# Sliding-window attention with sink keys and a swish feed-forward on one core: q and k put in token order by the read of PSUM, sink keys written by GpSimd, new constants in the planner

## The chip, the cores and the metric

One core of a Trainium2 chip runs the whole program. The metric is the device time of one execution in microseconds, on the slowest core; here there is only one. Five engines work side by side: TensorE (PE, with its weight load PEld), VectorE (DVE), ScalarE (ACT), GpSimd (POOL) and the queue engine SP, which here only issues DMAs. POOL and, once at the start, ACT issue DMAs too.

## The reference

Attention with 4 batches, 8 heads, 768 tokens and head size 64. A query sees the 4 first keys (the sinks) and the 128 keys up to itself. The result goes, token by token with all heads side by side, into a two-layer feed-forward.

```python
scores = scale * np.matmul(q, k.transpose(0, 1, 3, 2))
keep = is_sink | in_window
a = np.exp(np.where(keep, scores, -1e9) - max); a = a / a.sum()
x = (a @ v).transpose(0, 2, 1, 3).reshape(3072, 512)
h = x @ w_in                         # 512 -> 2048
g = h * (1.0 / (1.0 + np.exp(-beta * h)))
out = g @ w_out                      # 2048 -> 512
```

## The kernel before

The tokens are cut into 8 half-batches of 384 tokens (hb 0 to 7; two make a batch). A unit `u` is one pair of heads in one half-batch, so there are 32 units, 4 in each half-batch. The steps of a unit, each a function of `_program`:

- `load` and `cast`: q, k and v come by DMA as float32 and are cast to bf16 (`x16`, `vaug`) by DVE and ACT in hb 0, by POOL from then on. In the load of q and k a partition holds three consecutive tokens, so column block j of the cast tile holds the tokens 3s+j.
- `T` (line 420): six 128x128 transposes on PE put q and k of the unit into one PSUM bank, 768 columns of bf16 in the order (q or k, j, s). One copy (line 433, on ACT or DVE, whichever the planner holds to be free sooner) takes them to `qkT` in SBUF in token order (s, j): it reads the bank column by column and writes with a step of three elements. In an even half-batch two small copies by the same engine (line 440) put the 4 sink keys of each head into `kS`, a weight tile that is zero elsewhere: head 0 in the upper 64 rows at column 0, head 1 in the lower 64 rows at column 32.
- `SC` and `SS`: scores of the window blocks (8 matmuls over 4 banks) and of the sinks (one matmul with `kS` as weights); ACT takes the exponential (lines 489, 516), POOL masks the diagonal blocks with selects (line 495), DVE the sink block (line 503).
- `AV`: the weighted sum of v with a column of ones for the denominator; DVE divides (lines 555, 557, tile `onorm`). `OT`: three transposes back, copied to `xT` by ACT or DVE.

The feed-forward has 128 steps `H` (line 589: four matmuls of 384 columns, then tanh on ACT at line 593 and a product on DVE at line 595) and 96 steps `O` (line 607: four matmuls of 512 columns; every fourth ends a tile of 128 tokens, which is copied to `osb` and stored). An H step of a half-batch needs all four units of it.

The weights `w_in` and `w_out` come in four pieces each, by DMAs that POOL issues (line 384); all other loads are issued by SP. Loads are kept in order by `ordered`: a load waits until the load that lies `AHEAD_BYTES` back in the list `LOADS` has landed.

The order of everything is laid down when the program is built. `Graph` keeps a clock for each engine, `add` puts every instruction at a planned time from the cost that its caller gives (`act_ns`, `dve_ns`, `pool_ns`, `mm_ns`) and adds 180 ns where it waits for another engine. The loop at the end of `_program` (line 728) asks at each step which of OT, AV, SC, SS, T, H and O could start on PE, in this order, and takes the first that is ready by the planned clock, or else the one that is ready soonest. `background` (line 688) issues loads while the planned end of the DMAs is less than `BACKLOG` ahead, and casts. On the chip each engine then runs its instructions in that order and waits on semaphores.

Of the kernel before, what the change touches and what calls it, by code (L numbers as in the profile page):

```python
# [4 lines left out]
BF16 = mybir.dt.bfloat16  # L5
F32 = mybir.dt.float32
AF = mybir.ActivationFunctionType
ALU = mybir.AluOpType

B, H, S, D = 4, 8, 768, 64  # L10
NSINK, WINDOW = 4, 128
# [6 lines left out]
HALF = S // 2  # L18
# [209 lines left out]
def _program(nc, G, sb, ps, q, k, v, w_in, w_out, beta, out):  # L228
    NU = 2 * NPAIR
    NSTG, NX, NV, NT, NE, NON, NG, NTT, NOS, NKS = 2, 2, 3, 8, 3, 3, 3, 3, 4, 4  # L230
    NK = NB // 2
    ident = sb("ident", (128, 128), BF16)
    ones = sb("ones", (128, 128), BF16)
# [2 lines left out]
    ident32 = sb("ident32", (16, 16), F32)  # L236
    hbeta = sb("hbeta", (128, NM), F32)
    warm = sb("warm", (1, 1), F32)
    xT = sb("xT", (128, 4, NTOK), BF16)
    w_in16 = sb("w_in16", (128, 4, DF), BF16)  # L240
    w_out16 = sb("w_out16", (128, NM, NOUT), BF16)
# [5 lines left out]
    qkT = sb("qkT", (128, 2, HALF), BF16, NT)  # L247
    E = sb("E", (128, 6, 2, 128), BF16, NE)
    ES = sb("ES", (128, HALF), BF16, NE)
    kS = sb("kS", (128, 128), BF16, NKS)  # L250
# [8 lines left out]
    def add(eng, fn, ns, r=(), w=(), x=(), dma=None):  # L259
        return G.add(eng, fn, ns, r, w, x, dma)  # L260

    AHEAD_BYTES = 1600000

    def mm_ns(n):
        return max(n / 2.4, 25) + 3
# [30 lines left out]
    def take(n):  # L296
        got = choose(n)[1]
        held.update(got)
        return got
# [8 lines left out]
    def copy_fn(eng, dst, src, scale=1.0):  # L308
        if eng == "dve":
            if scale == 1.0:  # L310
                return lambda e: e.tensor_copy(dst, src)  # L311
            return lambda e: e.tensor_scalar(dst, src, scale, None, ALU.mult)
        return lambda e: e.activation(dst, src, AF.Copy, bias=0.0, scale=scale)  # L313


    def consts():
        add("gp", lambda e: e.memset(ones[:, :], 1.0), 150, w=["ones"])
        add("gp", lambda e: e.affine_select(ident[:, :], ones[:, :], [[1, 128]], ALU.is_equal, 0.0,
                                            base=0, channel_multiplier=-1), 250, r=["ones"], w=["ident"])
        add("gp", lambda e: e.affine_select(ident32[:, :], ones[0:16, 0:16], [[1, 16]], ALU.is_equal, 0.0,  # L320
                                            base=0, channel_multiplier=-1), 150, r=["ones"], w=["ident32"])
        for i in range(NV):
            add("gp", lambda e, i=i: e.memset(vaug[i][:, :, :, D:D + 1], 1.0), 50, w=[("vones", i)])
        for i in range(NKS):
            add("gp", lambda e, i=i: e.memset(kS[i][:, :], 0.0), 80, w=[("kS", i)])
        for i in range(2):
            add("gp", lambda e, i=i: e.memset(vS[i][:, :, :], 0.0), 350, w=[("vS", i)])
        for i, sg in ((0, 1), (1, -1)):
            add("gp", lambda e, i=i, sg=sg: e.affine_select(
                maskS[:, i, :], ones[:, :], [[sg, 128]], ALU.is_ge, 0.0, base=min(sg, 0), channel_multiplier=-sg),  # L330
                250, r=["ones"], w=[("maskS0", i)])
        add("gp", lambda e: e.affine_select(maskS[:, :, :], maskS[:, :, :], [[0, 2], [0, 128]], ALU.is_ge, 1.0,
                                            base=-NSINK, channel_multiplier=1), 400,
            r=[("maskS0", 0), ("maskS0", 1)], w=["maskS"])

        add("act", lambda e: e.activation(warm[:, :], ones[0:1, 0:1], AF.Exp, bias=0.0, scale=1.0), 1300,
            r=["ones"], w=["warm"])
# [12 lines left out]
    def ordered(nbytes):  # L350

        ahead, wait = 0, []
        for key, b_ in reversed(flight):
            ahead += b_
            if ahead > AHEAD_BYTES:
                wait = [key]
# [63 lines left out]
    def T(u):  # L420

        hb, hp = u // 4, u % 4
        bs = take(1)
        mp = P[:, bs[0], :].bitcast(BF16)
        for i, n in enumerate("qk"):
            for c in range(NK):
                add("pe", lambda e, i=i, n=n, c=c: nc.tensor.transpose(  # L427
                    mp[:, i * HALF + c * 128:i * HALF + (c + 1) * 128],
                    x16[n][hb % NX][:, c, 2 * hp:2 * hp + 2, :].rearrange("p h d -> p (h d)"), ident[:, :]),
                    mm_ns(128), r=[(n + "16", hb % NX, hp, c), "ident"], x=[("B", bs[0])])  # L430
        opts = {"dve": dve_ns(2 * HALF), "act": act_ns(2 * HALF)}
        eng = quickest(opts)
        add(eng, copy_fn(eng, qkT[u % NT][:, :, :].rearrange("p a (s j) -> p a j s", j=NK),
                         mp[:, 0:2 * HALF].rearrange("p (a j s) -> p a j s", a=2, j=NK)), opts[eng],
            w=[("qkT", u % NT)], x=[("B", bs[0])])
        if hb % 2 == 0:
            ks = u % NKS
            for hh in range(2):
                rows = slice(64 * hh, 64 * hh + 64)
                add(eng, copy_fn(eng, kS[ks][rows, 32 * hh:32 * hh + NSINK], qkT[u % NT][rows, 1, 0:NSINK]), 70,  # L440
                    r=[("kS", ks), ("qkT", u % NT)], w=[("kSd", ks, hh)])
        give(bs)


# [62 lines left out]
    def SS(u):  # L507

        b, half, hp = where(u)
        z, ks = u % NE, (u - 4 * half) % NKS  # L510
        q0 = 0 if half else 256
        bs = take(1)
        add("pe", lambda e: e.matmul(P[:, bs[0], q0:HALF], kS[ks][:, :], qkT[u % NT][:, 0, q0:HALF], start=True,  # L513
                                     stop=True), mm_ns(HALF - q0),
            r=[("kSd", ks, 0), ("kSd", ks, 1), ("qkT", u % NT)], x=[("B", bs[0])])
        add("act", lambda e: e.activation(ES[z][:, q0:HALF], P[:, bs[0], q0:HALF], AF.Exp, bias=0.0, scale=SCALE),  # L516
            act_ns(HALF - q0), w=[("ES", z)], x=[("B", bs[0])])
        give(bs)
# [113 lines left out]
    HS = [(T_, m) for T_ in range(NSB) for m in range(NM)]  # L632
    OS = [(T_, t, j) for T_ in range(NSB) for t in range(3) for j in range(4)]
    n_cast = [0]
    BACKLOG, AHEAD = 3000, 300

    def head(s):

# [89 lines left out]
    while True:  # L728
        background()
        now = G.free["pe"]  # L730
        if not started and done["T"] >= 2:
            beta_in()
            started = True
        ffn = ("O", "H") if last == "H" else ("H", "O")
        best = None
        for s in ("OT", "AV", "SC", "SS", "T") + ffn:
            h = head(s)
            if h is None:
                continue
            if h[0] <= now:  # L740
                best = (now, s, h[1])
                break
            if best is None or h[0] < best[0]:
                best = (h[0], s, h[1])
        if best is None:
            if done["O"] == len(OS):
                break
            G.free["pe"] = now + 200
            assert now < 1e6, (done, n_cast)
            continue  # L750
        _, s, fn = best
        if best[0] > now + 200:
            G.free["pe"] = now + 200
            continue
        fn()
        done[s] += 1
        if s in ("H", "O"):
            last = s
# [33 lines left out]
```

## Time and profile before

| what | us |
|---|---|
| median of 3 runs (lowest, highest) | 263.96 (263.18, 267.93) |
| the profiled execution | 265.0 |
| its span, first to last instruction | 263.2 |
| PE busy in it | 234.8 |
| ACT busy in it | 179.1 |
| DVE busy in it | 132.6 |
| POOL busy in it | 100.5 |

The 1.8 us between the profiled execution and its span lie outside the instructions. A busy PE is not a PE at its best rate: matmuls overlap, and the record of each is longer than the step from one to the next. So a stretch is read by the step between rows that follow one another, and by what stands at the same place when nothing is waited for.

### The profile page before, as it was taken

To read this page: it belongs to the slowest core of one execution; us is meant where nothing else is said; L and a number is where in the kernel's file an instruction comes from. 1 tells how busy PE (TensorE), PEld (TensorE's weight loads), DVE (VectorE), ACT (ScalarE), POOL (GpSimd) and SP (SyncE) were. 2 spreads that over 40 slices of the span, in tenths; PEclk is the share of its full clock that TensorE was granted. 3 is DMA by queue.
4 is the path that set the end of the run, shared out by engine and by line. 5 is a ranking of instruction groups with operands and counts; after the bars stand their busy time and mean duration, and the time that the engine had idled before them with its cause. 6 is when DMAs were issued, how large, how long until landed. Compare 5 with 4: busy or idle time off the path is not lost.

```text
span 263.2 us, 4995 instructions
## 1 busy us (share of the span) xinstructions
PE 234.8 (89%) x1889; PEld 132.6 (50%) x1889; DVE 132.6 (50%) x267; ACT 179.1 (68%) x307; POOL 100.5 (38%) x202
## 2 busy tenths in 40 slices
PE   1688977597899699988999999999999999999995
PEld 1354643363555466654556556555555555555542
DVE  1582751234584789455895344643443454353321
ACT  5884898339999478899879998745555564464420
POOL 5381559464774976967538255000000000000000
PEclk9999999899999799999999999999999999999999
DMA  6799995999999990970010101011111111111112
GB/s 200 159 160 201 273 197 95 209 264 295 186 280 256 265 278 18 294 135 0 5 40 4 42 0 42 0 40 42 40 40 45 40 40 42 40 40 40 42 41 80
DMA packets 49432, 29.69 MB, mean 113 GB/s; under 512 B 25840, under 2 KB 46336, under 8 KB 49408
## 3 DMA queue, kind: packets, MB, share of 16 engines
q1 hardware_dynamic: 44912, 24.98, 35.6%
q0 software_dynamic: 4224, 4.19, 10.0%
q8 instruction: 15, 0.25, 0.4%
q10 hardware_dynamic: 272, 0.20, 0.2%
q14 instruction: 9, 0.07, 0.1%
HBM read 27.27 MB, written 6.29 MB: 127 GB/s over the span
## 4 chain that ended last, share of the span: by engine, by line
PE 64%; ACT 21%; DVE 6%; DMA 4%; issue 1%; POOL 1%; SPq 0%; DVEq 0%; ACTq 0%
PE P L589 28%; PE P L607 26%; ACT qkT L313 9%; ACT E L489 6%; PE P L551 3%; DMA w_out<-in_moe_w_out_dram 3%; PE P L569 2%; ACT t L593 2%; PE P L479 2%; DVE g L595 2%; DMA k_stage<-in_k_dram 2%; DVE qkT L311 2%; DVE onorm L557 2%; ACT ES L516 1%; PE P L427 1%
## 5 line engine op out<-in xcount | busy, mean ns | idle before, releaser
L595 DVE SCALAR_TENSOR_TENSOR g<-t,P 128x384 bf16<-128x384 f32 x128 | 70.4, 554 | 88.8 <-ACT t L593 67.5
L593 ACT ACTIVATE t<-P,hbeta 128x384 f32<-128x384 f32 x128 | 74.3, 584 | 44.8 <-PE P L589 41.4
L607 PE MATMUL P<-w_out,g 128*128 128x512 bf16 x384 | 98.4, 382 | 4.3 <-DMA w_out<-in_moe_w_out_dram 2.2
L589 PE MATMUL P<-xT,w_in 128*128 128x384 bf16 x512 | 100.0, 333 | 0.4 <-DVE rden L555 0.4
L589 PEld LDWEIGHTS P<-xT,w_in 128*128 128x128 bf16 x512 | 50.0, 100 | 39.2 <-issue 3.3
L495 POOL TENSOR_SCALAR_AFFINE_SELECT E<-E 128x256 bf16<-128x256 bf16 (+1 forms) x112 | 51.6, 493 | 38.9 <-ACT E L489 38.6
L607 PEld LDWEIGHTS P<-w_out,g 128*128 128x128 bf16 x384 | 36.5, 98 | 39.9 <-DMA w_out<-in_moe_w_out_dram 2.9
L489 ACT ACTIVATE E<-P 128x768 bf16<-128x768 f32 x64 | 45.4, 773 | 5.6 <-PE P L479 5.5
L313 ACT ACTIVATE qkT<-P 128x768 bf16<-128x768 bf16 x20 | 28.8, 1486 | 1.1 <-PE P L427 1.1
L551 PE MATMUL P<-vaug,E 128*128 128x65 bf16 x352 | 20.9, 203 | 0.2 <-ACT vaug L313 0.2
L313 ACT ACTIVATE xT<-P 128x384 bf16<-128x384 bf16 x23 | 11.3, 498 | 13.7 <-PE P L569 13.6
L313 ACT ACTIVATE osb<-P 128x512 f32<-128x512 f32 x20 | 12.1, 604 | 12.3 <-PE P L607 12.3
L479 PE MATMUL P<-qkT 64*128 64x128 bf16 (+1 forms) x256 | 17.8, 251 | 2.2 <-ACT E L489 0.9
L551 PEld LDWEIGHTS P<-vaug,E 128*128 128x128 bf16 x352 | 18.5, 104 | 2.3 <-issue 0.6
L557 DVE TENSOR_TENSOR onorm<-P,rden 128x384 bf16<-128x384 f32 x32 | 17.8, 558 | 1.1
L311 DVE COPY qkT<-P 128x768 bf16<-128x768 bf16 x12 | 17.4, 1448 | 0.4 <-PE P L427 0.4
L569 PE MATMUL P<-ident,onorm 128*128 128x128 bf16 x96 | 11.3, 233 | 6.9 <-DVE onorm L557 5.9
L407 POOL TENSOR_SCALAR_AFFINE_SELECT vaug<-v_stage 128x512 bf16<-128x512 f32 x21 | 13.6, 667 | 5.3 <-DMA v_stage<-in_v_dram 5.3
L479 PEld LDWEIGHTS P<-qkT 64*128 64x128 bf16 x256 | 8.8, 97 | 12.2 <-issue 3.7
L541 PE MATMUL P<-vS,ES 128*128 128x130 bf16 x64 | 13.7, 233 | 0.2
L569 PEld LDWEIGHTS P<-ident,onorm 128*128 128x128 bf16 x96 | 6.7, 102 | 13.5 <-DVE onorm L557 9.2
L516 ACT ACTIVATE ES<-P 128x128 bf16<-128x128 f32 (+1 forms) x32 | 12.9, 409 | 1.0 <-PE P L513 0.8
(46 smaller groups left out, 130.4 us busy)
## 6 DMA issues: line engine op xcount, KB each, us to landing
v_stage<-in_v_dram SPq DMA_DIRECT2D x24, 256.0 KB, 5.8
out_dram<-osb SPq DMA_DIRECT2D x24, 256.0 KB, 2.0
q_stage<-in_q_dram SPq DMA_DIRECT2D x7, 768.0 KB, 6.0
k_stage<-in_k_dram SPq DMA_DIRECT2D x7, 768.0 KB, 7.1
w_in<-in_moe_w_in_dram POOLq DMA_DIRECT2D x4, 512.0 KB, 5.5
w_out<-in_moe_w_out_dram POOLq DMA_DIRECT2D x4, 512.0 KB, 6.7
q_stage<-in_q_dram SPq DMA_DIRECT2D x4, 192.0 KB, 4.0
k_stage<-in_k_dram SPq DMA_DIRECT2D x3, 192.0 KB, 4.9
```

Source lines behind the costliest of these rows:

```text
L311: return lambda e: e.tensor_copy(dst, src)
L313: return lambda e: e.activation(dst, src, AF.Copy, bias=0.0, scale=scale)
L479: add("pe", lambda e, dst=dst, kt=kt, kc=kc, rows=rows, q0=q0, nq=nq: e.matmul(dst, kt[rows, 1, kc:kc + 128], qkT[u % NT][rows, 0, q0:q0 + ...
L489: add("act", lambda e, src=src, dst_=dst_: e.activation(dst_, src, AF.Exp, bias=0.0, scale=SCALE), act_ns(256 * n), w=[(k_, z, j) for k_ i ...
L495: add("gp", lambda e, d=d, sg=sg, at_=at_: e.affine_select(d, d, [[0, 2 * len(at_)], [sg, 128]], ALU.is_ge, 0.0, base=min(sg, 0), channel_ ...
L551: e.matmul(A[:, c0:c0 + D + 1], E[z][:, i, hh, :], vaug[vz][:, kb % NK, 2 * hp + hh, :], start=a, stop=o, skip_group_check=True), 39,
L557: add("dve", lambda e: e.tensor_tensor(onorm[on][:, :, :, :].rearrange("p m h d -> p (m h) d"), av[:, :, 0:D], rden[on][:, :].unsqueeze(2) ...
L569: add("pe", lambda e, m=m: nc.tensor.transpose(mp[:, m * 128:(m + 1) * 128], onorm[on][:, m, :, :].rearrange("p h d -> p (h d)"), ident[:, ...
L589: add("pe", lambda e, c=c: e.matmul(hp, w_in16[:, c, m * 128:(m + 1) * 128], xT[:, c, t0:t0 + HALF], start=(c == 0), stop=(c == 3)), mm_ns ...
L593: add("act", lambda e: e.activation(tt[ti][:, :], hp, AF.Tanh, bias=0.0, scale=hbeta[:, m:m + 1]), act_ns(HALF) + 93, r=["hbeta"], w=[("t" ...
L595: add("dve", lambda e: e.scalar_tensor_tensor(gt[T_ % NG][:, m, :], tt[ti][:, :], 1.0, hp, ALU.add, ALU.mult), dve_ns(HALF), r=[("t", ti)] ...
L607: add("pe", lambda e, m=m: e.matmul(P[:, bk, :], gt[T_ % NG][:, m, t * 128:(t + 1) * 128], w_out16[:, m, :], start=(m == 0), stop=(m == NM ...
```

## The change

- The PSUM-to-SBUF copy in `T` now writes `qkT` in one run and takes the permutation on its input: three neighbours in the output are read 128 columns apart in PSUM.
- The two small copies into `kS` go. One POOL multiply writes both heads at once, 128 rows x 2 x 4: the sink keys, read twice, times `headm`, a mask of 128x2 that is 1 for the upper rows in its first column and for the lower rows in its second. `SS` waits for it.
- `AHEAD_BYTES` goes from 1.6 to 3.2 MB and `BACKLOG` from 3000 to 6000 ns.
- With `MARGIN` = 200 ns an attention step is only taken at once if it has been ready for 200 ns, and a later kind of step in the list is taken if it is ready 200 ns sooner than the best so far, or H or O if they are ready.

```diff
-    AHEAD_BYTES = 1600000
+    AHEAD_BYTES = 3200000
...
+        for i, sg in ((0, -1), (1, 1)):
+            add("gp", lambda e, i=i, sg=sg: e.affine_select(
+                headm[:, i:i + 1], ones[:, 0:1], [[0, 1]], ALU.is_ge, 0.0, base=63 if i == 0 else -64,
+                channel_multiplier=sg), 110, r=["ones"], w=["headm"] if i else ["headm0"])
...
-        add(eng, copy_fn(eng, qkT[u % NT][:, :, :].rearrange("p a (s j) -> p a j s", j=NK),
-                         mp[:, 0:2 * HALF].rearrange("p (a j s) -> p a j s", a=2, j=NK)), opts[eng],
+        add(eng, copy_fn(eng, qkT[u % NT][:, :, :].rearrange("p a (s j) -> p a s j", j=NK),
+                         mp[:, 0:2 * HALF].rearrange("p (a j s) -> p a s j", a=2, j=NK)), opts[eng],
             w=[("qkT", u % NT)], x=[("B", bs[0])])
         if hb % 2 == 0:
             ks = u % NKS
-            for hh in range(2):
-                rows = slice(64 * hh, 64 * hh + 64)
-                add(eng, copy_fn(eng, kS[ks][rows, 32 * hh:32 * hh + NSINK], qkT[u % NT][rows, 1, 0:NSINK]), 70,
-                    r=[("kS", ks), ("qkT", u % NT)], w=[("kSd", ks, hh)])
+            kd = kS[ks][:, :].rearrange("p (a w) -> p a w", w=32)[:, 0:2, 0:NSINK]
+            add("gp", lambda e: e.tensor_tensor(
+                kd, qkT[u % NT][:, 1:2, 0:NSINK].to_broadcast([128, 2, NSINK]),
+                headm[:, :].unsqueeze(2).to_broadcast([128, 2, NSINK]), ALU.mult), 200,
+                r=[("kS", ks), ("qkT", u % NT), "headm"], w=[("kSd", ks)])
...
-    BACKLOG, AHEAD = 3000, 300
+    BACKLOG, AHEAD, MARGIN = 6000, 300, 200
...
-            if h[0] <= now:
+            if h[0] + (MARGIN if s in ("OT", "AV", "SC", "SS", "T") else 0) <= now:
                 best = (now, s, h[1])
                 break
-            if best is None or h[0] < best[0]:
+            if best is None or h[0] + MARGIN < best[0]:
                 best = (h[0], s, h[1])
```

The planner's new order differs in many places. Three of them, on the two engines that the prediction speaks of most:

POOL, from the casts of hb 1 to the first selects after them (`w_out` rows are DMA issues, `E` rows the selects, `q_1`, `k_1` and `vaug` the casts). Before:

```order
L407 AFFINE_SELECT q_1<-q_stage 128x512 x3
L384 DMA w_out<-in_moe_w_out_dram 128x4x512
L407 AFFINE_SELECT k_1<-k_stage 128x512 x3
L407 AFFINE_SELECT vaug<-v_stage 128x8x64
L384 DMA w_out<-in_moe_w_out_dram 128x4x512
L407 AFFINE_SELECT vaug<-v_stage 128x8x64 x2
L384 DMA w_out<-in_moe_w_out_dram 128x4x512
L495 AFFINE_SELECT E<-E 128x256
L495 AFFINE_SELECT E<-E 128x512 x2
L495 AFFINE_SELECT E<-E 128x256 x2
L495 AFFINE_SELECT E<-E 128x512 x2
L495 AFFINE_SELECT E<-E 128x256
```

After:

```order
L389 DMA w_out<-in_moe_w_out_dram 128x4x512
L412 AFFINE_SELECT q_1<-q_stage 128x512 x3
L389 DMA w_out<-in_moe_w_out_dram 128x4x512
L412 AFFINE_SELECT k_1<-k_stage 128x512 x3
L412 AFFINE_SELECT vaug<-v_stage 128x8x64
L389 DMA w_out<-in_moe_w_out_dram 128x4x512
L412 AFFINE_SELECT vaug<-v_stage 128x8x64 x2
L389 DMA w_out<-in_moe_w_out_dram 128x4x512
L501 AFFINE_SELECT E<-E 128x256
L501 AFFINE_SELECT E<-E 128x512 x2
L501 AFFINE_SELECT E<-E 128x256 x2
L501 AFFINE_SELECT E<-E 128x512 x2
```

All four issues of `w_out` stand one place earlier: the first is ahead of the casts of q, and the last, which stood behind the first two units' selects (the row after the piece shown), is now ahead of them.

POOL again, at the casts of hb 2, which starts the second batch. Before:

```order
L407 AFFINE_SELECT q_0<-q_stage 128x512 x3
L407 AFFINE_SELECT k_0<-k_stage 128x512 x3
L407 AFFINE_SELECT vaug<-v_stage 128x8x64 x3
L407 AFFINE_SELECT q_1<-q_stage 128x512 x3
L495 AFFINE_SELECT E<-E 128x256 x3
```

After:

```order
L412 AFFINE_SELECT q_0<-q_stage 128x512 x3
L412 AFFINE_SELECT k_0<-k_stage 128x512 x3
L412 AFFINE_SELECT vaug<-v_stage 128x8x64 x2
L444 TENSOR_TENSOR kS<-qkT,headm 128x2x4 x2
L412 AFFINE_SELECT vaug<-v_stage 128x8x64
L444 TENSOR_TENSOR kS<-qkT,headm 128x2x4 x2
L412 AFFINE_SELECT q_1<-q_stage 128x512 x3
```

The four sink tiles of hb 2 are written behind two and three of its casts of v, which wait for DMAs of their own.

PE at the same place, from the last transposes of hb 2 (`T`) over the sink scores (`kS` rows) to the scores of its first two units. Before:

```order
L427 MATMUL P<-ident,q_0 128x128 x3
L427 MATMUL P<-ident,k_0 128x128 x3
L607 MATMUL P<-w_out,g 128x512 x4
L513 MATMUL P<-qkT,kS 128x128
L589 MATMUL P<-xT,w_in 128x384 x4
L513 MATMUL P<-qkT,kS 128x128 x2
L607 MATMUL P<-w_out,g 128x512 x4
L589 MATMUL P<-xT,w_in 128x384 x4
L607 MATMUL P<-w_out,g 128x512 x4
L479 MATMUL P<-qkT 128x256 x2
L479 MATMUL P<-qkT 128x128 x6
```

After:

```order
L432 MATMUL P<-ident,q_0 128x128 x3
L432 MATMUL P<-ident,k_0 128x128 x3
L595 MATMUL P<-xT,w_in 128x384 x4
L519 MATMUL P<-qkT,kS 128x128
L613 MATMUL P<-w_out,g 128x512 x4
L519 MATMUL P<-qkT,kS 128x128 x2
L595 MATMUL P<-xT,w_in 128x384 x4
L613 MATMUL P<-w_out,g 128x512 x4
L595 MATMUL P<-xT,w_in 128x384 x4
L613 MATMUL P<-w_out,g 128x512 x4
L485 MATMUL P<-qkT 128x256 x2
L485 MATMUL P<-qkT 128x128 x6
```

The first sink score still stands one feed-forward step behind the transposes; the scores stand one H step later. Counted over the whole program, the first T of hb 2 to the last OT held 44 H and 30 O steps before and holds 59 and 39 now; behind the last OT there were 66 H and 58 O, and there are 53 and 48. The counts of H and O ahead of hb 2's T were 18 and 8 and are 16 and 9. Of the 32 copies to `qkT` ACT has 20 and DVE 12, before and after.

## Rows read from the trace of the kernel before

**Rows 1.** Stretches of the span: busy us of each engine (instructions), granted clock, DMA share
```profile
4.40:21.60 17.20, 12.30 (x118) 7.79 (x119) 10.48 (x25) 13.60 (x27) 8.17 (x17) 1.00 0.93 180
21.60:34.40 12.80, 12.80 (x66) 7.07 (x65) 7.62 (x14) 9.08 (x16) 4.86 (x8) 1.00 1.10 236
34.40:58.60 24.20, 18.26 (x175) 10.17 (x173) 7.58 (x16) 13.92 (x21) 15.58 (x29) 0.93 0.92 195
58.60:165.60 107.00, 97.47 (x1038) 59.02 (x1036) 67.81 (x143) 92.91 (x161) 68.30 (x132) 0.98 0.53 132
165.60:263.20 97.60, 93.97 (x501) 48.54 (x499) 38.65 (x70) 47.89 (x83) 0.00 (x0) 1.00 0.11 41
```

**Rows 2.** Chain that ended last, feed-forward alone: start, length, what
```profile
248.66 0.65 PE P L589 x4
249.31 0.86 PE P L607 x4
...
260.14 0.60 ACT osb L313
```

**Rows 3.** Timeline of PE, two places in the attention: start, length, what
```profile
81.34 0.45 PE L479 MATMUL P<-qkT 64*128 64x256 bf16 x8
81.73 0.34 PE L427 MATMUL P<-ident,q_1 128*128 128x128 bf16 x3
81.91 0.33 PE L427 MATMUL P<-ident,k_1 128*128 128x128 bf16 x3
...
103.30 0.33 PE L569 MATMUL P<-ident,onorm 128*128 128x128 bf16 x3
103.47 0.22 PE L541 MATMUL P<-vS,ES 128*128 128x130 bf16 x1
...
104.01 0.22 PE L513 MATMUL P<-qkT,kS 128*128 128x128 bf16 x1
104.06 0.81 PE L589 MATMUL P<-xT,w_in 128*128 128x384 bf16 x4
```

**Rows 4.** Groups by line and shape: total busy us, mean ns, idle before
```profile
L593 ACT ACTIVATE t<-P,hbeta 128x384 f32<-128x384 f32 x128 | 74.3, 584 | 44.8 <-PE P L589 41.4
L489 ACT ACTIVATE E<-P 128x768 bf16<-128x768 f32 x48 | 37.6, 824 | 5.6 <-PE P L479 5.5
L495 POOL TENSOR_SCALAR_AFFINE_SELECT E<-E 128x256 bf16<-128x256 bf16 x80 | 33.6, 436 | 38.9 <-ACT E L489 38.6
L313 ACT ACTIVATE qkT<-P 128x768 bf16<-128x768 bf16 x20 | 28.8, 1486 | 1.1 <-PE P L427 1.1
L557 DVE TENSOR_TENSOR onorm<-P,rden 128x384 bf16<-128x384 f32 x32 | 17.8, 558 | 1.1
L311 DVE COPY qkT<-P 128x768 bf16<-128x768 bf16 x12 | 17.4, 1448 | 0.4 <-PE P L427 0.4
L311 DVE COPY kS<-qkT 64x4 bf16<-64x4 bf16 x20 | 5.2, 260 | 0.5
L313 ACT ACTIVATE kS<-qkT 64x4 bf16<-64x4 bf16 x12 | 2.4, 204 | 0.4
```

**Rows 5.** Chain that ended last, start to 51 us: start, length, what
```profile
7.75 1.46 ACT qkT L313
...
9.73 1.30 ACT E L489 x2
...
35.18 3.90 ACT qkT L313 x3
...
44.21 6.62 DMA w_out<-in_moe_w_out_dram
```

**Rows 6.** The two stretches at a lower granted clock, columns as in rows 1
```profile
50.40:53.80 3.40, 2.91 (x20) 1.72 (x21) 0.69 (x2) 0.00 (x0) 1.43 (x3) 0.50 0.75 224
...
88.00:91.30 3.30, 2.77 (x23) 2.05 (x24) 2.76 (x6) 0.98 (x2) 3.30 (x7) 0.50 1.19 256
```

**Rows 7.** Waits of PE, 58.6 to 165.6 us: us in total, times, longest
```profile
PE P L569 <- DVE onorm L557: 3.7, 5, 1.8
PE P L513 <- ACT kS L313: 1.4, 2, 1.1
```

More of the change, by code (lines that the diff above doesn't have):

```diff
@@ L238, in _program @@
     warm = sb("warm", (1, 1), F32)
+    headm = sb("headm", (128, 2), BF16)
     xT = sb("xT", (128, 4, NTOK), BF16)
@@ L514, in SS @@
                                      stop=True), mm_ns(HALF - q0),
-            r=[("kSd", ks, 0), ("kSd", ks, 1), ("qkT", u % NT)], x=[("B", bs[0])])
+            r=[("kSd", ks), ("qkT", u % NT)], x=[("B", bs[0])])
         add("act", lambda e: e.activation(ES[z][:, q0:HALF], P[:, bs[0], q0:HALF], AF.Exp, bias=0.0, scale=SCALE),
```

## Prediction

> **What bounds the kernel now.** I read the span by stretches first, cut where the kind of work changes [rows 1]. Behind 165.6 us there is only feed-forward, and PE does it without a gap: an H step takes 0.65 us, an O step 0.86 us [rows 2]. The 66 H and 58 O steps left there make 66 x 0.65 + 58 x 0.86 = 92.8 us of the 97.6; the other 4.8 us are the last transposes, the end of the last chain, the last copy (0.60 us, rows 2) and its store. Nothing in this change makes such a step shorter. What it can do is to get more of these steps done earlier, in gaps that PE has now.
>
> So the question is how much PE loses ahead of 165.6 us. The busy column doesn't say it, since records of matmuls overlap; I price PE's work by steps between rows. A unit's scores take 0.39 us (81.34 to 81.73), its two halves of T 0.18 each (0.36), OT 0.17, the weighted sum in an odd half-batch 0.54 (103.47 to 104.01) and a sink score 0.05 [rows 3]. In an even half-batch the weighted sum has 11 matmuls in place of 15, 0.36 by my estimate; a sink score over 384 columns is taken like one H matmul, 0.16.
>
> From the first T of hb 2 (58.6) to the last OT (165.6) stand 24 units: T 8.6, scores 9.4, weighted sums 12 x 0.54 + 12 x 0.36 = 10.8, OT 3.9, sinks 2.5, together 35.2 us; with 44 H (28.6) and 30 O (25.8) that is 89.6 us of work in 107.0 us. PE loses 17.4 us there. In the stretch from 34.4 to 58.6 the same prices give 4 units at 1.62 (6.5), 8 O (6.9) and 2 H (1.3), 14.7 of 24.2 us: 9.5 us lost. ACT is busy 92.9 of the 107.0 us, 87%, the most of any engine but PE [rows 1].
>
> The groups by line show where ACT's time goes: 20 copies to `qkT` at 1486 ns, against 824 ns for an exponential of as many columns out of PSUM, whose output runs on in order. DVE's 12 copies take 1448 ns, while a product of half as many columns out of PSUM takes 558 ns [rows 4]. Both engines need about 1.8 times as long as their neighbours of the same size, and the step of three in the output is what these copies have and the neighbours lack.
>
> **The change part by part.** *The copies.* On ACT the nearest row is the exponential: 0.82 us, a saving of 0.66 each. On DVE 768 columns cost less than twice the 558 ns of 384, so under 1.12; I take 0.95, a saving of 0.50. No row shows a read of PSUM with a step. Its ends are 0.82 and 1.49 us on ACT, 0.70 (under one cost of 384 columns and a half more) and 1.45 on DVE. I take the fast ends, since the columns and the engine are the same as in the exponential's row.
>
> [...]
>
> *The sink copies.* 12 on ACT (2.4 us) and 20 on DVE (5.2 us) go [rows 4]. POOL gets 16 multiplies of 8 columns; no row shows one. A select of 256 columns takes 0.44 us, so 0.44 is the upper end, 0.1 the lower; I take 0.25, 4 us over the program on an engine that is busy 68.3 of 107.0 us [rows 1]. This is hidden unless PE stands at a sink score. In hb 4 and hb 6 the scores come several steps after T; in hb 2 they stand one step behind it, and there POOL's casts of v, and the DMAs they wait for, are queued ahead. I put 1 to 1.5 us on that, once, of which the waits for the sink copies of today (1.4 us, rows 7) pay for nearly all.
>
> *Start, to 21.6 us.* The second copy and its sink copies stand on the chain from 7.75 to 9.73 us [rows 5]; 0.66 and about 0.4 us go. Against that the first piece of `w_in` may now be loaded beside the last q, k and v, at a DMA share of 0.93 [rows 1]. I take a gain of 1.0 us, ends 2.5 and -1.5.
>
> *34.4 to 58.6 us.* Three copies on the chain, 3.90 us [rows 5], become 3 x 0.82 = 2.46: 1.4 us. Then the chain waits 6.62 us for the last piece of `w_out`, whose issue stood behind the selects of two units, and now stands ahead of them. The piece comes sooner, but not at once: the same bytes must come, and the DMA share of 0.93 and 0.92 in the first and third stretch against 1.10 in the second leaves room for 17.2 x 0.17 + 24.2 x 0.18 = 7.3 us of transfers at most. I take 4.0 us off PE's wait, ends 1 and 6.6. [...] Together 5.4 us. So the first T of hb 2 starts at 58.6 - 1.0 - 5.4 = 52.2; I say 52.5 us, ends 50 and 56.5. Its casts need q and k of hb 2 about as much earlier, which the same room allows.
>
> *52.5 us to the last OT.* The order puts 59 H and 39 O steps there: 38.4 + 33.5 + 35.2 = 107.1 us of PE work. ACT's load falls by the copies (15 x 1.49 to 14 x 0.82, 10.8 us) and the sink copies, and rises by 15 tanh at 0.58 [rows 4], 8.7 us: about the same work over a longer stretch. DVE loses 10 copies x 0.50 and 20 x 0.26 less what lies in hb 0, some 9 us; that helps the divisions behind which OT waits (3.7 us, rows 7). The planner charged a copy with half of what it took, and now with nearly all, so its order fits better, and a step that must have been ready for 200 ns leaves PE waiting less. The wait for a division also stands ahead of the second stretch at half clock [rows 6], where up to 1.65 us were lost. Of the 17.4 us lost I take 9 as left, an estimate: about half. Ends are 17.4 (what PE waits for is other than the copies) and 5.
>
> *The sum.* 52.5 + 107.1 + 9 + 53 x 0.65 + 48 x 0.86 + 4.8 = 249.1 us of span, against 263.2. With the 1.8 us outside the span the profiled execution would take 250.9; it was 265.0, 1.0 us above the median of the three runs, so I say 250.0 us for a median.
>
> **The rivals.** *A: a stepped read of PSUM costs as much as the stepped write* (the change then doesn't do what it says). For it: both engines lose 0.65 to 0.86 ns too much for each element, so a memory may be what is slow, and the step moves to a memory that has not been tried. Against it: no row with PSUM as input is slow in itself. Then the copies' part of the start and of the second stretch is lost (0.7 and 1.4 us) and T of hb 2 comes at 54.6, the loss stays 17.4 us, and the span is 54.6 + 107.1 + 17.4 + 80.5 = 259.6; 260.4 us for a median. [...]
>
> *B: the copies are fast and the loads set the pace.* A DMA share of 1.10 may be all there is, and 0.93 all that small pieces allow. Then T of hb 2 stays at 57.6 and the rest is as forecast: 254.2 of span, 255.0 us.
>
> *C, slower: POOL's queue holds up the sink scores.* Place: `SS`, which PE runs in order, behind the multiply, which stands behind selects and casts that themselves wait for ACT or a DMA. Price: three selects are 1.31 us; if each of the 16 units in even half-batches waits that long, 21 us are added to 250: 271 us. It eats the gain from 14 / 16 = 0.9 us a unit, and is slower by 2% from 1.2 us a unit. For it: today PE waited up to 1.1 us for a sink copy [rows 7]. Against it: in hb 4 and 6 the order leaves several steps between T and `SS`.
>
> **How the numbers follow.** Forecast 0.60, A 0.22, B 0.10, C 0.08. A measurement of this kernel can tell about 2% from no change, so faster means below 258.7 us and slower above 269.2. Faster: nearly all of the forecast and B, and a fifth of A, 0.74; same: the rest of A and B, 0.17; slower: C and a little of A (worse copies than before, or a start held up by loads), 0.09. The low end is T at 50 with 5 us lost, 242.6 of span, 243.4 us; the high end T at 56.5 with the whole loss, 261.5 of span, 262.3 us, which holds A and B and leaves out C.
>
> **What would show it.** Right: `qkT` copies near 0.82 and 0.95 us; the last `w_out` wait gone or below 2.6 us; T of hb 2 at 52 to 53; the last OT near 169, behind which PE runs without a gap for 80 us; at most one short stretch at half clock. Wrong: copies at 1.4 us or more (A); T of hb 2 behind 56 with PE waiting for q or k casts (B); PE waiting for `kS` for more than 0.5 us at many units (C); or PE still losing 15 us or more in the mixed stretch though the copies are fast, which would say that they were not what it waited for.

## The result and the profile after

| what | before | after |
|---|---|---|
| median, us (lowest, highest) | 264.11 (263.18, 267.93), 4 runs | 249.28 (247.13, 250.54), 4 runs |
| ratio to before, with 95% interval | 1 | 0.9441 (0.9347 to 0.9536) |
| profiled execution, us | 265.0 | 250.16 |
| its span, us | 263.2 | 248.4 |

Executions more than 1.5% above the fastest of their kernel count in the medians here and below, but not in the ratios: of e3's four (median 253.80) that leaves 248.80 and 252.28, and the profiled execution of r_after (250.97) is one of those left out.

The forecast was 250.0 us and a span of 249.1. The sum came out, but two of its terms were wrong by about 3 us with opposite signs: its close fit is in part luck. The two terms show as soon as the span is cut at the same places as before: first H, first T of hb 1, first T of hb 2, last OT. The windows of the changed kernel, with the columns of [rows 1]:

```profile
4.40:25.80 21.40, 11.32 (x117) 7.93 (x118) 8.40 (x22) 11.90 (x23) 9.41 (x21) 1.00 1.14 246
25.80:38.00 12.20, 12.20 (x64) 6.71 (x62) 7.08 (x13) 8.52 (x15) 8.51 (x13) 1.00 1.00 179
38.00:55.30 17.30, 15.70 (x171) 9.31 (x173) 7.21 (x17) 11.90 (x21) 12.23 (x24) 1.00 1.01 248
55.30:168.20 112.90, 109.80 (x1118) 68.21 (x1133) 67.11 (x140) 92.53 (x172) 69.99 (x143) 1.00 0.46 122
168.20:248.40 80.20, 76.15 (x400) 39.51 (x406) 30.87 (x56) 38.01 (x65) 0.00 (x0) 1.00 0.12 43
```

Read against [rows 1], the first stretch is 4.2 us longer, the third 6.9 us shorter, and the mixed stretch holds 24 more feed-forward steps than before and is only 5.9 us longer. Priced as in the prediction its work is 107.1 us, so PE loses 112.9 - 107.1 = 5.8 us there, against 17.4. Behind the last OT 80.2 us are left against 97.6. No stretch of this execution has a granted clock below 1.00; the two of [rows 6] are gone. (When the same kernel ran again, one was there: r_after, below.)

The groups by line that answer to [rows 4]:

```profile
L314 ACT ACTIVATE qkT<-P 128x768 bf16<-128x768 bf16 x20 | 16.2, 828 | 1.4 <-PE P L432 1.4
L312 DVE COPY qkT<-P 128x768 bf16<-128x768 bf16 x12 | 11.3, 952 | 1.8 <-PE P L432 1.6
L444 POOL TENSOR_TENSOR kS<-qkT,headm 128x8 bf16<-128x8 bf16 x16 | 3.3, 211 | 6.1 <-ACT qkT L314 5.8 <-DVE qkT L312 0.3
L495 ACT ACTIVATE E<-P 128x768 bf16<-128x768 f32 x48 | 37.3, 819 | 6.8 <-PE P L485 6.8
```

ACT's copy fell from 1486 to 828 ns, about as long as the exponential of as many columns (819); DVE's from 1448 to 952. The multiply on POOL takes 211 ns.

What made the first stretch longer stands in the timeline of the changed kernel (start, length, engine, line, what; in brackets the idle time ahead and what ended it):

```profile
4.82 0.95 POOL L389 DMA_DIRECT2D w_in<-in_moe_w_in_dram  x1
...
9.03 1.31 POOL L501 TENSOR_SCALAR_AFFINE_SELECT E<-E 128x256 bf16<-128x256 bf16 x3 [1.25 <-ACT E L495]
10.29 0.78 POOL L389 DMA_DIRECT2D w_in<-in_moe_w_in_dram  x1
11.09 0.21 POOL L444 TENSOR_TENSOR kS<-qkT,headm 128x8 bf16<-128x8 bf16 x1
...
11.36 0.29 PE L519 MATMUL P<-qkT,kS 128*128 128x128 bf16 x1 [1.42 <-POOL kS L444]
...
13.06 0.63 ACT L314 ACTIVATE vaug<-v_stage 128x512 bf16<-128x512 f32 x1 [1.27 <-DMA v_stage<-in_v_dram]
...
15.06 0.63 ACT L314 ACTIVATE vaug<-v_stage 128x512 bf16<-128x512 f32 x1 [1.37 <-DMA v_stage<-in_v_dram]
...
19.19 0.43 DVE L312 CAST vaug<-v_stage 128x512 bf16<-128x512 f32 x1 [5.01 <-DMA v_stage<-in_v_dram]
...
19.67 0.68 PE L557 MATMUL P<-vaug,E 128*128 128x65 bf16 x9 [3.42 <-DVE vaug L312]
```

The first piece of `w_in` is issued at 4.82 us, while v of hb 0 is still under way. The third block of v can be cast at 19.19 us. It is that late in this execution only: in six other traces with the deeper loads, among them one of this very kernel (r_after), the last cast of v starts at 15.0 to 15.8 us. Before, ACT cast all three by 15.2 us and waited for none of them:

```profile
12.21 0.63 ACT L313 ACTIVATE vaug<-v_stage 128x512 bf16<-128x512 f32 x1
...
13.90 0.65 ACT L313 ACTIVATE vaug<-v_stage 128x512 bf16<-128x512 f32 x1
...
14.57 0.66 ACT L313 ACTIVATE vaug<-v_stage 128x512 bf16<-128x512 f32 x1
```

Of PE's waits over the whole span (in total, times, longest) these answer to [rows 7]:

```profile
PE P L557 <- DVE vaug L312: 3.4, 1, 3.4
PE P L557 <- ACT vaug L314: 2.5, 2, 1.7
PE P L575 <- DVE onorm L563: 1.8, 4, 0.9
PE P L519 <- POOL kS L444: 1.4, 1, 1.4
```

In the mixed stretch alone no wait is longer than 0.6 us, and the wait for a division there went from 3.7 us in five [rows 7] to 0.3 in one.

### The profile page after: what moved, and what is told of

It reads as the page before. It is cut to its first block, busy times and chain, and to the rows that moved or that the text cites. A ratio compares the mean times of both kernels' runs of the same rounds, so it can differ in the third digit from the quotient of the medians.

```text
span 248.4 us, 4941 instructions
## 1 busy us (share of the span) xinstructions
PE 225.2 (91%) x1862; PEld 131.7 (53%) x1889; DVE 121.0 (49%) x246; ACT 164.4 (66%) x296; POOL 103.7 (42%) x220
## 4 chain that ended last, share of the span: by engine, by line
PE 78%; ACT 7%; DMA 5%; DVE 3%; SPq 2%; issue 2%; POOL 1%; DVEq 0%
PE P L595 33%; PE P L613 30%; DMA v_stage<-in_v_dram 5%; PE P L557 4%; PE P L485 3%; ACT E L495 3%; PE P L432 3%; PE P L575 2%; SPq L379 2%; ACT qkT L314 1%; ACT t L599 1%; PE P L547 1%; DVE g L601 1%; DVE onorm L563 1%; PE P L519 1%
## 5 line engine op out<-in xcount | busy, mean ns | idle before, releaser
L601 DVE SCALAR_TENSOR_TENSOR g<-t,P 128x384 bf16<-128x384 f32 x128 | 69.8, 554 | 80.5 <-ACT t L599 67.0
L613 PE MATMUL P<-w_out,g 128*128 128x512 bf16 x357 | 92.4, 379 | 2.7 <-ACT ES L522 0.7
L557 PE MATMUL P<-vaug,E 128*128 128x65 bf16 x352 | 20.0, 199 | 6.7 <-DVE vaug L312 3.4
L557 PEld LDWEIGHTS P<-vaug,E 128*128 128x128 bf16 x352 | 17.5, 101 | 10.1 <-DVE vaug L312 3.6
L314 ACT ACTIVATE osb<-P 128x512 f32<-128x512 f32 x22 | 13.2, 598 | 13.5 <-PE P L613 13.2
L314 ACT ACTIVATE qkT<-P 128x768 bf16<-128x768 bf16 x20 | 16.2, 828 | 1.4 <-PE P L432 1.4
L485 PE MATMUL P<-qkT 64*128 64x128 bf16 (+1 forms) x256 | 16.6, 251 | 0.1
L547 PE MATMUL P<-vS,ES 128*128 128x130 bf16 x64 | 13.0, 225 | 0.0
L312 DVE COPY qkT<-P 128x768 bf16<-128x768 bf16 x12 | 11.3, 952 | 1.8 <-PE P L432 1.6
L575 PEld LDWEIGHTS P<-ident,onorm 128*128 128x128 bf16 x96 | 7.4, 101 | 8.0 <-DVE onorm L563 2.5
```

The costliest lines, as they stand in the source:

```text
L485: add("pe", lambda e, dst=dst, kt=kt, kc=kc, rows=rows, q0=q0, nq=nq: e.matmul(dst, kt[rows, 1, kc:kc + 128], qkT[u % NT][rows, 0, q0:q0 + ...
L547: add("pe", lambda e, m=m, c0=c0: e.matmul(A[:, c0:c0 + 2 * (D + 1)], ES[z][:, m * 128:(m + 1) * 128], vS[b % 2][:, 2 * hp:2 * hp + 2, :]. ...
L557: e.matmul(A[:, c0:c0 + D + 1], E[z][:, i, hh, :], vaug[vz][:, kb % NK, 2 * hp + hh, :], start=a, stop=o, skip_group_check=True), 39,
L575: add("pe", lambda e, m=m: nc.tensor.transpose(mp[:, m * 128:(m + 1) * 128], onorm[on][:, m, :, :].rearrange("p h d -> p (h d)"), ident[:, ...
L601: add("dve", lambda e: e.scalar_tensor_tensor(gt[T_ % NG][:, m, :], tt[ti][:, :], 1.0, hp, ALU.add, ALU.mult), dve_ns(HALF), r=[("t", ti)] ...
L613: add("pe", lambda e, m=m: e.matmul(P[:, bk, :], gt[T_ % NG][:, m, t * 128:(t + 1) * 128], w_out16[:, m, :], start=(m == 0), stop=(m == NM ...
```

## The experiments

For all of them one table, cut as above (us of the profiled execution). "Lost" is the mixed stretch less its work, with the prices of the prediction and the H and O steps that the order puts there. Each ratio is to runs of the kernel before on the same chip. r_after is the changed kernel once more.

| kernel | first H | T of hb 2 | last OT | H, O in between | lost | median | ratio (95%) |
|---|---|---|---|---|---|---|---|
| before | 21.6 | 58.6 | 165.6 | 44, 30 | 17.4 | 264.11 | 1 |
| after | 25.8 | 55.3 | 168.2 | 59, 39 | 5.8 | 249.28 | 0.944 (0.935 to 0.954) |
| r_after: after again | 22.0 | 56.1 | 169.0 | 59, 39 | 5.8 | 248.89 | 0.941 (0.931 to 0.950) |
| e2: copy alone | 20.2 | 54.5 | 153.9 | 44, 30 | 9.8 | 253.24 | 0.960 (0.953 to 0.968) |
| e1: all but the copy | 22.8 | 54.3 | 171.7 | 59, 39 | 10.3 | 253.63 | 0.961 (0.955 to 0.967) |
| m1: margin alone | 20.8 | 60.1 | 180.6 | 57, 41 | 13.0 | 260.75 | 0.986 (0.980 to 0.991) |
| m2: copy and margin | 20.2 | 54.8 | 167.9 | 57, 41 | 5.6 | 249.95 | 0.951 (0.945 to 0.957) |
| e3: all but the margin | 21.5 | 53.8 | 150.4 | 43, 28 | 9.4 | 253.80 | 0.950 (0.939 to 0.961) |
| l1: loads alone | 22.4 | 54.7 | 160.3 | 48, 30 | 13.4 | 257.14 | 0.978 (0.974 to 0.981) |
| e5: all but the loads | 18.9 | 54.2 | 163.0 | 55, 38 | 5.2 | 247.69 | 0.937 (0.930 to 0.945) |
| e4: v ahead of w_in | 20.9 | 56.1 | 161.7 | 55, 35 | 4.6 | 249.27 | 0.945 (0.940 to 0.950) |
| e6: all but the sinks | 22.8 | 53.9 | 170.0 | 61, 41 | 6.0 | 249.68 | 0.945 (0.939 to 0.951) |
| e7: measured costs | 21.8 | 55.7 | 181.6 | 71, 47 | 4.1 | 247.92 | 0.939 (0.932 to 0.947) |
| b1: e5 and e7 | 19.5 | 52.6 | 179.4 | 70, 47 | 5.7 | 248.36 | 0.946 (0.943 to 0.950) |

### The copies: e1 and e2

e1 takes the copy back in the changed kernel; the order of the instructions stays that of after.

```diff
-        add(eng, copy_fn(eng, qkT[u % NT][:, :, :].rearrange("p a (s j) -> p a s j", j=NK),
-                         mp[:, 0:2 * HALF].rearrange("p (a j s) -> p a s j", a=2, j=NK)), opts[eng],
+        add(eng, copy_fn(eng, qkT[u % NT][:, :, :].rearrange("p a (s j) -> p a j s", j=NK),
+                         mp[:, 0:2 * HALF].rearrange("p (a j s) -> p a j s", a=2, j=NK)), opts[eng],
```

> The changed kernel with one edit undone: the copy to qkT writes with a step of three again and reads PSUM in order. The order of all engines is that of the changed kernel to the row. Theory F (the copies are what PE waited for in the mixed stretch): copies back at 1.45 to 1.49 us, the loss of PE from the first T of hb 2 to the last OT goes from 5.8 to 14 us or more, 1 to 2 us come back ahead of it; 257 to 262 us. Theory G (loads issued earlier and the planner's margin gave the gain, the copies were beside it): at most 2 us above the changed kernel, 249 to 252 us.

e2 is the same edit the other way round: the kernel before, in its own order, with the new copy and nothing else.

> The kernel before with the new copy alone: qkT written in order, PSUM read with a step; the order of all engines is that of before. Theory F: copies at 0.83 and 0.95 us, 0.7 us gained at the start, 1.4 us at the three copies ahead of the w_out wait (though that wait then takes it back), and some 6 to 9 us in the mixed stretch; 253 to 257 us. Theory G: 261 to 264 us.

The groups by line, of e1:

```profile
L314 ACT ACTIVATE qkT<-P 128x768 bf16<-128x768 bf16 x20 | 28.8, 1482 | 1.0 <-PE P L432 1.0
L312 DVE COPY qkT<-P 128x768 bf16<-128x768 bf16 x12 | 17.2, 1447 | 2.0 <-PE P L432 1.9
```

and of e2:

```profile
L313 ACT ACTIVATE qkT<-P 128x768 bf16<-128x768 bf16 x20 | 15.9, 823 | 1.3 <-PE P L427 1.2
L311 DVE COPY qkT<-P 128x768 bf16<-128x768 bf16 x12 | 11.4, 952 | 0.4 <-PE P L427 0.4
```

The duration follows the copy's form in either order, so it is the step in the write that costs some 660 ns on ACT (1482 and 1486 against 823 and 828) and 495 on DVE (1447 and 1448 against 952), and on ACT the copy with the step in the read takes 6 and 9 ns more than the exponential of as many columns (823 against 817 in e2, 828 against 819 in after). The copy alone is worth 4.0%, with every instruction in the place that it had before. From T of hb 2 to the last OT e2 runs the same H, O and attention steps as before in 99.4 us in place of 107.0 (last row of its windows); by estimate 1.7 of these 7.6 us are the second stretch of [rows 6], 3.3 us at a granted clock of 0.50, counted half (in e5 an O step takes 1.71 us at 0.50 and 0.88 at 1.00), which e2 doesn't have:

```profile
20.20:32.90 12.70, 12.70 (x66) 7.02 (x65) 7.60 (x14) 9.08 (x16) 5.27 (x9) 1.00 1.17 245
32.90:54.50 21.60, 16.19 (x173) 9.57 (x173) 7.01 (x16) 12.22 (x21) 13.80 (x26) 1.00 1.03 204
54.50:153.90 99.40, 94.28 (x1025) 58.46 (x1038) 66.58 (x143) 85.51 (x162) 69.50 (x134) 1.00 0.57 145
```

The part of the change that is not the copy is worth 3.9% (e1). Neither theory had this: 253.63 us lies between their times, and the loss of 10.3 us is less than the 14 of theory F. 4.0 and 3.9 don't add up to the 5.6 of the whole: the two overlap.

### The margin: m1, m2 and e3

m1 is the kernel before with the margin alone, m2 has the new copy as well, e3 is the changed kernel without it.

```diff
-    BACKLOG, AHEAD = 3000, 300
+    BACKLOG, AHEAD, MARGIN = 3000, 300, 200
...
-            if h[0] <= now:
+            if h[0] + (MARGIN if s in ("OT", "AV", "SC", "SS", "T") else 0) <= now:
...
-            if best is None or h[0] < best[0]:
+            if best is None or h[0] + MARGIN < best[0]:
```

> The kernel before with MARGIN = 200 ns alone: stepped writes, sink copies and load settings as before. The run with the stepped write in the changed order was 10 us faster than before without the fast copies, so something of sinks, loads and margin gives that. If it is the margin: 253 to 256 us, and a loss in the mixed stretch near the 10.3 us of that run. If the margin only pays together with the loads or the sinks: 260 us or more.

> The kernel before with the new copy and the margin, and nothing else (sink copies and load settings as before). If the whole gain is these two: 247 to 250 us, no more than 1.5 us from the changed kernel. If sinks or loads are needed: 251 us or more.

In e3 the last two lines stay, with:

```diff
-    BACKLOG, AHEAD, MARGIN = 6000, 300, 200
+    BACKLOG, AHEAD, MARGIN = 6000, 300, 0
```

> The changed kernel with MARGIN = 0, all else the same; the order changes, with 37 in place of 48 O and 59 in place of 75 H steps ahead of the last OT. Theory F: the copies give most and the margin 1 to 3 us; 250 to 253 us. Theory G: the margin is half of the gain or more; 256 us or more.

The column "lost" tells it. Without either, 17.4 us; the margin alone 13.0, and e1, which has it too, 10.3; the copy without the margin 9.8 (e2) and 9.4 (e3); both together 5.6 (m2) and 5.8 (after and r_after). So the margin takes 4.4, 4.2 and 3.6 us off the loss (before to m1, e2 to m2, e3 to after). The copy takes 7.6 and 7.4 with the loads of before (before to e2, m1 to m2), but only 4.5 with the deeper ones, in the same order of instructions (e1 to after): the deeper loads alone take off 4.0 (l1), and nothing more once the copy and the margin are there (m2 against after). By time, the margin alone is the second case of its expectation (260.75 us). The copy and the margin (0.951) are nearly the whole change (0.944); their intervals overlap, so what the rest adds is not told apart from nothing. Nor is the time that the margin adds to all the rest (e3, 0.950): it shows in the loss alone. The orders without the margin have 43 to 48 H steps there, those with it 55 and more: with a margin the planner puts an H step in where an attention step has only just come ready, and that step would have its input by the time that PE comes to it. No run followed this step by step, so this reason is argued and not shown.

### The loads: l1, e5 and e4

l1 is the kernel before with the deeper loads alone; e5 the changed kernel with the loads of before, by this edit (l1 has it the other way round):

```diff
-    AHEAD_BYTES = 3200000
+    AHEAD_BYTES = 1600000
...
-    BACKLOG, AHEAD, MARGIN = 6000, 300, 200
+    BACKLOG, AHEAD, MARGIN = 3000, 300, 200
```

> The kernel before with AHEAD_BYTES 3.2 MB and BACKLOG 6000 ns alone. The changed kernel with these two taken back was no slower, so alone they should give little: 261 to 265 us. If they give what the margin does not, 254 to 258 us.

> The changed kernel with AHEAD_BYTES and BACKLOG back at 1.6 MB and 3000 ns; copies, sink tiles and margin as changed. If loads issued earlier matter, T of hb 2 comes at 56 us or later and the time is 252 us or more. If the transfers themselves are the pace there (every kernel so far with any part of the change has that T at 53.8 to 56.1 us), the setting is worth under 1 us: 248 to 250.5 us.

Alone the deeper loads gave 2.2%, more than was expected of them. In the changed kernel taking them back costs nothing: 0.937 is the lowest ratio of all, though its interval overlaps that of the change. e5 has v in time. Its casts of v, in the timeline:

```profile
11.28 1.19 ACT L314 ACTIVATE vaug<-v_stage 128x512 bf16<-128x512 f32 x2
...
12.72 0.62 DVE L312 CAST vaug<-v_stage 128x512 bf16<-128x512 f32 x1
```

The first H stands at 18.9 us, 6.9 ahead of after, and T of hb 2 at 54.2, only 1.1 ahead. The windows of e5 between show where the head start went:

```profile
29.60:33.00 3.40, 2.64 (x36) 1.87 (x33) 2.19 (x4) 2.36 (x5) 3.39 (x6) 1.00 1.20 190
33.00:36.00 3.00, 0.43 (x3) 0.12 (x2) 0.02 (x1) 3.00 (x6) 0.05 (x1) 0.87 1.24 204
36.00:38.00 2.00, 1.95 (x6) 0.57 (x8) 0.00 (x0) 0.14 (x1) 1.87 (x4) 0.50 0.62 108
38.00:40.00 2.00, 2.00 (x25) 1.49 (x22) 0.20 (x1) 1.51 (x2) 1.99 (x5) 0.50 0.00 1
40.00:42.00 2.00, 2.00 (x9) 0.55 (x9) 0.56 (x2) 0.49 (x1) 2.00 (x4) 0.50 0.86 130
```

From 33 to 36 us PE has three matmuls: it waits for `w_out`, as in [rows 5], and from 36 to 42 the granted clock is 0.50, as in [rows 6]. In after that wait is gone and PE is full from 25.8 us on (12.20 of 12.20 us up to 38.0), but it starts later. That goes with the late start, not with the setting alone: with the deeper loads and an earlier start the wait is there in r_after (3.0 us), e3 (1.6), e6 (2.4 in two), e7 (3.4 in two) and l1 (1.9), and 0.3 in e1. The last piece of `w_out` lands at 46.8 us in after and at 47.0 in r_after; PE comes to it at 48.9 and at 44.0. One wait is traded for the other.

e4 goes for both: the changed kernel, but no piece of `w_in` is issued before the first unit's scores are placed.

```diff
-                    load_w(x)
-                    done["load"] += 1
-                    moved = True
+                    if done["SC"] >= 1:
+                        load_w(x)
+                        done["load"] += 1
+                        moved = True
```

> The changed kernel, but the first piece of w_in is issued only when the planner has placed the first unit's scores, so POOL issues it behind that unit's selects, at about 9 to 10 us in place of 4.8. Theory S (the start is 4 us later than before because that piece shares the DMA engines with the v loads of hb 0): the last v piece lands 3 to 4 us sooner, the first H step starts at 20.5 to 22.5 in place of 25.8 us, and the time is 244 to 247 us. Rival: v lands as late as with the changed kernel, since the DMAs behind it are what is slow; first H at 25 to 26 and 249 us.

The third block of v lands at 11.8 us, against 19.2 in after and 15.0 in r_after. The first H comes 4.9 us sooner than in after and 1.1 sooner than in r_after, T of hb 2 not at all (56.1 against 55.3 and 56.1), and the time is that of after, not the 244 to 247 us of theory S. The waits of POOL in e4, 20 to 56 us:

```profile
POOL w_out L389 <- DMA w_in<-in_moe_w_in_dram: 8.6, 1, 8.6
POOL vaug L412 <- DMA v_stage<-in_v_dram: 6.2, 1, 6.2
```

POOL's queue stands for 8.6 us at the issue of `w_out`, which keeps its distance to `w_in`. That is nothing of e4's own: it stands there for 8.1 to 8.4 us in r_after, e1, e3, e6 and l1, and for 5.1 and 6.4 in after and e7. The 6.2 us at v of hb 1 are e4's own; what was held back at the start is missing there, and PE waits 3.3 us for selects that are queued behind.

### The sink copies: e6

The changed kernel with the two small copies of before in place of POOL's multiply.

```diff
-            kd = kS[ks][:, :].rearrange("p (a w) -> p a w", w=32)[:, 0:2, 0:NSINK]
-            add("gp", lambda e: e.tensor_tensor(
-                kd, qkT[u % NT][:, 1:2, 0:NSINK].to_broadcast([128, 2, NSINK]),
-                headm[:, :].unsqueeze(2).to_broadcast([128, 2, NSINK]), ALU.mult), 200,
...
+            for hh in range(2):
+                rows = slice(64 * hh, 64 * hh + 64)
+                add(eng, copy_fn(eng, kS[ks][rows, 32 * hh:32 * hh + NSINK], qkT[u % NT][rows, 1, 0:NSINK]), 70,
+                    r=[("kS", ks), ("qkT", u % NT)], w=[("kSd", ks, hh)])
```

> The changed kernel with the sink keys copied by ACT or DVE again, two small copies a unit in even half-batches, and no POOL multiply; the rest as changed. 24 units of such copies beside hb 0 and hb 2 cost ACT and DVE some 7 us of busy time over the program. Forecast theory: that lies beside other work, 249 to 251 us. Rival: POOL's queue holds up the sink scores in the changed kernel, and this is faster, 246 to 248 us.

0.945 with the small copies and 0.944 with the multiply: the edit is worth nothing that can be measured, though the order shifts with it (61 and 41 steps in place of 59 and 39). Neither the work that it takes from ACT and DVE nor the queue on POOL shows in the time.

### A planner with measured costs, and the change once more: e7, b1 and r_after

After, the planner charges ACT with n/1.2 + 60 ns and DVE with n/rate + 65; with the part that goes by n kept, the rows of after leave 188 and 152 (828 and 952 ns for 768 elements, less 640 and 800), taken as 180 and 150.

```diff
-        return n / 1.2 + 60
+        return n / 1.2 + 180
...
-        return n / rate + 65
+        return n / rate + 150
```

> The changed kernel whose planner charges what the rows show: 180 ns fixed for an ACT instruction in place of 60, 150 ns for one of DVE in place of 65. If an order that fits the chip's durations is what the copies and the margin brought, this loses less than 5.8 us in the mixed stretch: 245 to 248 us. If the rest of that loss is not of the order's making, 249 us; and more, if the longer charges only push work behind the attention.

b1 has this and the loads of before.

> The version that the runs point to: the changed kernel with the load settings of before and the planner's charges for ACT and DVE taken from the rows (180 and 150 ns fixed). Each alone was 1 us or so faster than the changed kernel, inside the interval. If they add up: 245.5 to 247.5 us; if the loads of the first 55 us are the bound of both: 247.5 to 248.5 us.

> The changed kernel once more, beside the others of this series on one chip: 248 to 250.5 us. If its start varies from run to run with the landing of the v loads of hb 0, its first H step is not at 25.8 us again but somewhere from 21 to 26.

e7 puts 71 H and 47 O steps into the mixed stretch and loses the least there, 4.1 us. Its 247.92 us lie within the interval of after, and so does b1: the points of e5 and e7 don't add up. The change itself, run again, had 248.89 us, ratio 0.9405 (0.931 to 0.9501), with single runs from 247.17 to 253.68. Which of after, e5, e7 and b1 is fastest is within that spread and stays open.

The trace of r_after shows what of the changed kernel repeats and what doesn't. From its timeline and its windows (first H, T of hb 1 to T of hb 2, mixed stretch):

```profile
14.97 0.43 DVE L312 CAST vaug<-v_stage 128x512 bf16<-128x512 f32 x1 [0.54 <-DMA v_stage<-in_v_dram]
...
47.04 1.89 PE L613 MATMUL P<-w_out,g 128*128 128x512 bf16 x4 [3.03 <-DMA w_out<-in_moe_w_out_dram]
```

```profile
4.40:21.98 17.58, 11.43 (x117) 7.83 (x118) 8.60 (x22) 11.93 (x23) 9.38 (x21) 1.00 1.15 250
...
33.13:56.09 22.96, 18.66 (x174) 10.27 (x172) 7.44 (x18) 11.89 (x21) 15.96 (x30) 0.85 1.06 241
56.09:169.01 112.92, 110.77 (x1134) 68.23 (x1133) 66.42 (x138) 92.56 (x172) 69.59 (x142) 1.00 0.44 117
```

The mixed stretch repeats, to 112.9 us with 5.8 lost. The start doesn't: v is cast 4.2 us sooner and the first H stands at 22.0 us, where the expectation had 21 to 26. What is gained there is lost again ahead of hb 2, where PE waits 3.03 us for the last piece of `w_out` and the granted clock is 0.50 from 45.3 to 52.1 us, so that T of hb 2 comes at 56.1.

## Why the prediction was right, point by point

**The copies** were taken at 0.82 and 0.95 us and have 828 and 952 ns. That the step in the write was the cause, read from neighbours of the same size in [rows 4], holds (e1, e2). Rival A falls with them: it had the copies stay at 1.49 and 1.45 us.

**The start** was off: a gain of 1.0 us, ends 2.5 and -1.5, where the profile of the result has a loss of 4.2. In r_after the same kernel loses 0.4, inside the ends. The copies' part was real: with the loads of before, the kernels that have the new copy begin H at 18.9 to 20.2 us (e5, b1, e2, m2), against 21.6 before and 20.8 in m1. What was mis-sized is the piece of `w_in` beside the last v, to which the prediction gave 1.5 us at most. Where that piece is issued at 9.9 us or later, the third block of v lands at 11.5 to 12.4 us (before, e2, e4, e5, m1, m2, b1); where it is issued at 4.5 to 4.8 us, at 15.0 to 15.8 (r_after, e1, e3, e6, e7, l1), some 3 us later. e4 has the deeper loads without the early piece, so it is the piece. In after the block landed at 19.2 us, 12.69 us after its issue, in the chain of waits (start, length, what):

```profile
5.35 1.08 SPq L379
6.48 12.69 DMA v_stage<-in_v_dram
```

With the deeper loads first H stands at 21.5 to 22.8 us in those six traces, and at 25.8 in after alone. e1, in the same order and with slower copies, has 22.8. So some 3 to 4 of the 4.2 us are what that one execution had; what made its v so late is open.

**34.4 to 58.6 us** was to get 5.4 us shorter. The moved issue brought the last piece of `w_out` in 4.1 us sooner (46.8 in place of 50.8 us; 3.9 in r_after), as forecast. But the forecast took 4.0 us off PE's wait, and the 6.62 us of [rows 5] are the flight of that DMA; PE itself waited 2.2 us. Its waits for `w_out` before (34.4 to 58.6 us) and in r_after (33.13 to 56.09 us; in total, times, longest):

```profile
PE P L607 <- DMA w_out<-in_moe_w_out_dram: 2.2, 2, 1.5
...
PE P L613 <- DMA w_out<-in_moe_w_out_dram: 3.0, 1, 3.0
```

In after the wait is gone, since PE came later than the piece, and no stretch at a granted clock of 0.50 stands behind it. T of hb 1 to T of hb 2 fell by 6.9 us, and H ahead of it by 0.6. So T of hb 2 came at 55.3, within the ends of 50 and 56.5, but not at 52.5: the start was 5.2 us later than forecast, these two stretches 2.1 us shorter, and 0.3 had been added in rounding. In r_after, with the start nearly in time, the two are 2.5 us longer than forecast and T of hb 2 comes at 56.1. So it is 2.8 or 3.6 us late, by either way.

**Rival B**, that the loads set the pace ahead of hb 2, was too late with its 57.6 us, but right in that gains ahead of hb 2 don't all arrive there. The copy alone, the loads alone, and any mix of the parts bring T of hb 2 to between 52.6 and 56.1; only before and the margin alone are later. The landing of the last piece of `w_out` goes with it: 44.8 to 48.9 us in all of these, 50.8 and 51.1 in those two. Wherever a wait was taken away at the start, another came before hb 2 (e4, e5, r_after). The DMA share is 1.14, 1.00 and 1.01 in the three windows of after up to 55.3 us. That the sum of bytes is what holds it there fits all of this, but no run took bytes away, so it is argued and not shown.

**The mixed stretch** was to lose 9 us and loses 5.8. The mechanism was right: the copies alone leave 9.8 (e2). The margin was taken for a part of that half; it is worth another 4 us (m2 against e2, after against e3). This term was 3.2 us too high, and covered the 2.8 us at T of hb 2: that the two are of one size is luck.

**Behind the last OT**: 80.5 us forecast, 80.2 measured, at 168.2 us where "near 169" was said. Counting steps in the new order was enough.

**Rival C** falls. PE waits for `kS` once, 1.42 us, of the size forecast; but in hb 0, behind three selects and an issue of `w_in` (11.36 us in the timeline), not in hb 2, where it doesn't wait. e6, without the multiply, waits 1.37 us at the same place, for a small copy on DVE. The multiply has 211 ns where 250 were taken.

## What to carry to other kernels

When a copy takes much too long on two different engines, compare it with a neighbour of the same size whose access is in one run, and try the permutation on the other side: here that took 0.66 us off each of 20 copies and 0.50 off 12, and 4.0% off the kernel without moving one instruction. Gains don't add up where they fill the same gaps: three parts that gave 4.0, 2.2 and 1.5% alone gave 5.6 together. They overlapped ahead of hb 2, where the last weights land at 44.8 to 48.9 us whichever part is in, and behind it, where the copy and the deeper loads took off the same loss. A load that is issued earlier can delay the one that is needed first, here v by some 3 us. In an order that is planned ahead, a margin of 200 ns on "ready" took about 4 us off PE's loss. And one trace of a kernel is one execution: the late start of after was not there when it ran again.

## What the runs showed that was not expected

The copy that reads PSUM in bf16 with a step of 128 elements took ACT about as long as the exponential that reads in one run (828 ns for 768 elements, against 819; DVE has no copy of that size in one run beside its 952), while the one that writes SBUF in bf16 with a step of three elements took 1.8 times as long on ACT (1482 ns in e1, against 828) and 1.5 times on DVE (1447 against 952).

One early DMA of weights went with a block of v that landed some 3 us later in six traces (15.0 to 15.8 us, against 11.5 to 12.4 in the seven without it), and 7 us later in one (19.2).

Small copies on DVE took longer beside work of POOL. The 20 copies into `kS` have a mean of 260 ns before [rows 4] and 399 in e2, in the same order, with nothing else changed but the big copies:

```profile
L311 DVE COPY kS<-qkT 64x4 bf16<-64x4 bf16 x20 | 8.0, 399 | 0.5
```

The traces of the six kernels with such copies (before, l1, m1, e2, m2, e6) tell where the time goes. The 25 of them beside which POOL does nothing take 159 to 168 ns. Of the 77 that take more than 200 ns, 72 end 17 to 22 ns after a select or a cast of POOL has ended; the other five stand at the start, beside a DMA issue of POOL. In e2, for example, a cast ends at 59.52 us, and the first of two copies, 599 ns long, at 59.54:

```profile
58.86 0.66 POOL L407 TENSOR_SCALAR_AFFINE_SELECT vaug<-v_stage 128x512 bf16<-128x512 f32 x1 [0.38 <-DMA v_stage<-in_v_dram]
58.94 0.78 DVE L311 COPY kS<-qkT 64x4 bf16<-64x4 bf16 x2
```

In e2 19 of the 20 copies meet work of POOL, before 14 did. This hurt where PE stood behind it: in e2 the sink score at 59.77 us waits 1.20 us for these two copies.
